# Sharing an attention kernel's exponentials between ScalarE and VectorE, in an order computed at build time

## Chip, cores and metric

The kernel runs on one core of one Trainium2 chip. The metric is the device time of one execution in microseconds (us), the median of several executions. The engines are PE (TensorE), ACT (ScalarE), DVE (VectorE) and POOL (GpSimd); PEld is PE's weight load, SP starts DMA transfers. PSUM is the memory that PE writes its sums to, in banks of 128x512 numbers here; the other engines read them from there. The profile adds, for one execution, every instruction's start and length and the clock that PE was granted (1.0 is full speed).

An execution is called slow when it lies more than 1.5% above the fastest one of the same kernel. Ratios below are the mean time of one kernel's fast runs over that of the kernel before in the same rounds, so they differ a little from the ratio of the medians that are quoted.

## The reference

A multi-head attention block and a bilinear feed-forward block read the same `x` (2048 x 512, bf16), and a sigmoid gate per row mixes them.

```python
g = sigmoid((x * gate_w).sum(-1, keepdims=True))
q, k, v = split(x @ wqkv)                  # 32 heads of 16 columns
p = softmax(q @ k.T * 16 ** -0.5)          # 32 heads x 2048 x 2048
a = (p @ v) @ wo
b = ((x @ w_gate) * (x @ w_up)) @ w_down   # 512 -> 1376 -> 512
out = g * a + (1 - g) * b
```

Softmax needs 32 x 2048 x 2048 exponentials. The matmuls of the feed-forward block and the projections need no exponentials and are used to fill PE's free time ("fills").

## The kernel before

Scores are computed transposed (keys on partitions, 512 queries in the free dimension), four heads at a time, each in its own strip of 32 rows of PE. A *score group* is four heads x 128 keys x 512 queries, four blocks of 128x512; there are 512 groups. Three blocks make a *span*: three score matmuls into three PSUM banks, then one exponential over 1536 columns by ScalarE. Two slots of three banks alternate. PV matmuls (probabilities times V) sum one group in four column strips of one bank; V carries columns of ones, so the softmax denominator comes out beside the result.

```python
def exp(i):                                   # every exponential is ScalarE's
    u0, n = spans[i]                          # n = 3 blocks, 2 in the last head group
    o_exp[i] = P.op("act", lambda a: a.activation(
        PT[:, r0 : r0 + n, :]..., psS[:, slot[i] : slot[i] + 512 * n], ACT.Exp, scale=0.25), deps)

def pv(e):                                    # one PV group: four heads side by side
    for j in range(4):
        pe.matmul(psO[32*j : 32*j+32, :], Vp[:, kt, 8*b + 2*j + p, :], PT[:, cell[4*e+j], :],
                  start=(kt == 0), stop=(kt == T - 1), tile_position=(0, 32*j))

for i in range(len(spans)):                   # the order: a fixed pattern with credits
    exp(i)
    scores(i + 2)
    ...                                       # PV of what is ready
    rate = 4.0 if first else (2.0 if chunk == 0 else 1.3)
    credit = min(credit + rate, 4.0)          # at most this many fill matmuls a span
    ...
```

The softmax here doesn't subtract the row's maximum and nothing guards it: scores larger than these inputs give would overflow.

## Time and profile before

The kernel before takes 1002.07 us (median of 4 runs, 994.84 to 1008.29).

| what | value |
|---|---|
| ScalarE busy | 94% of 998.0 us |
| exponentials of 1536 columns, start to start | 1.345 us |
| exponentials of 1024 columns, start to start | 0.917 us |
| PE busy / mean granted clock | 79% / 0.838 |
| VectorE busy | 16% |

The first fence is from the page of the kernel before: busy us by engine (with the share of the 998.0 us span), the busy share in 40 equal slices (digits are tenths; PEclk is the granted PE clock in tenths), and the chain of work and waits that ended last, by engine (a q marks an engine's sequencer).

```profile
PE 786.5 (79%) x5072; PEld 187.9 (19%) x5072; DVE 159.1 (16%) x260; ACT 939.2 (94%) x713; POOL 50.3 (5%) x41
...
PE   3787788888888787788877788778778777777797
...
DVE  1333332122211111111011112110000100000001
ACT  2677799999999999999999999999999999999998
...
PEclk9998899999997999998999999998557955555557
...
ACT 61%; issue 17%; PE 14%; DVE 4%; DMA 2%; SPq 0%; ACTq 0%; DVEq 0%
```

ScalarE is at 9 in nearly every slice after the start and makes up 61% of the chain that ended last: it is the bound. PE's clock, the PEclk row, falls to half speed in the last quarter while ScalarE stays at 9.

The next fence has groups of instructions by form: line, engine, operation, output and input tile, shapes, count, then busy us and mean ns of one, then idle time before them and its releaser. After it come two rows of the chain of waits in order of time (start, length, and a merged run of large exponentials), then a timeline row of ScalarE with small ones.

```profile
L541 ACT ACTIVATE PT<-psS 128x1536 bf16<-128x1536 f32 x661 | 894.4, 1688 | 44.7 <-PE psS L520 44.2
L520 PE MATMUL psS<-QT,KE 32*128 32x512 bf16 x2048 | 319.4, 455 | 156.3 <-ACT PT L541 144.0 <-DVE KE L275 1.7 <-DVE QT L296 0.8
...
L541 ACT ACTIVATE PT<-psS 128x1024 bf16<-128x1024 f32 x32 | 30.2, 1022 | 2.9 <-PE psS L520 2.9
```

```profile
827.70 4.03 ACT PT L541 x3
833.07 9.41 ACT PT L541 x7
```

```profile
956.87 3.77 ACT L541 ACTIVATE PT<-psS 128x1024 bf16<-128x1024 f32 x4 [0.38 <-PE psS L520]
```

One large exponential lasts 1688 ns but overlaps the next: in the chain seven take 9.41 us and three 4.03 us, so (9.41 - 4.03) / 4 = 1.345 us from start to start. Four small ones take 3.77 us, so (3.77 - 1.02) / 3 = 0.917 us. PE sat idle for 144.0 us before score matmuls, waiting for exponentials, but ScalarE for only 47 us waiting for PE.

The last view is busy time by stretch of the span: the stretch, its length, then for PE, PEld, DVE, ACT and POOL busy us and instruction count, then PE clock, DMA share and GB/s.

```profile
0.00:100.00 100.00, 66.33 (x435) 18.18 (x435) 30.49 (x53) 61.25 (x45) 12.32 (x11) 0.95 0.37 88
100.00:700.00 600.00, 488.99 (x3274) 123.25 (x3271) 112.35 (x176) 587.72 (x436) 26.59 (x21) 0.95 0.04 12
...
800.00:850.00 50.00, 38.05 (x226) 7.17 (x226) 1.89 (x4) 50.00 (x39) 2.53 (x2) 0.50 0.04 12
```

The first 100 us cost 39 us of ScalarE time. From 100 us on ScalarE is 98 to 100% busy in these stretches (95% in the first 100 us of them), at the full clock and at the half clock alike (800 to 850 us: clock 0.50, ScalarE 50.00 of 50.00 us).

### The profile page before, as it was taken

To read this page: it belongs to the slowest core of one execution; us is meant where nothing else is said; L and a number is where in the kernel's file an instruction comes from. 1 tells how busy PE (TensorE), PEld (TensorE's weight loads), DVE (VectorE), ACT (ScalarE), POOL (GpSimd) and SP (SyncE) were. 2 spreads that over 40 slices of the span, in tenths; PEclk is the share of its full clock that TensorE was granted. 3 is DMA by queue.
4 is the path that set the end of the run, shared out by engine and by line. 5 is a ranking of instruction groups with operands and counts; after the bars stand their busy time and mean duration, and the time that the engine had idled before them with its cause. 6 is when DMAs were issued, how large, how long until landed. Compare 5 with 4: busy or idle time off the path is not lost.

```text
span 998.0 us, 11864 instructions
## 1 busy us (share of the span) xinstructions
PE 786.5 (79%) x5072; PEld 187.9 (19%) x5072; DVE 159.1 (16%) x260; ACT 939.2 (94%) x713; POOL 50.3 (5%) x41
## 2 busy tenths in 40 slices
PE   3787788888888787788877788778778777777797
PEld 0222122222222222222212122121111111111111
DVE  1333332122211111111011112110000100000001
ACT  2677799999999999999999999999999999999998
POOL 4000000000000000000000000000000000000000
PEclk9998899999997999998999999998557955555557
DMA  7600000000000000000000000000000000000000
GB/s 147 191 12 1 12 12 11 3 11 12 12 12 23 22 4 9 12 12 12 13 12 22 12 11 12 12 12 12 1 11 17 28 12 12 12 1 11 12 12 21
DMA packets 29980, 19.91 MB, mean 20 GB/s; under 512 B 19464, under 2 KB 24936, under 8 KB 29928
## 3 DMA queue, kind: packets, MB, share of 16 engines
q1 hardware_dynamic: 26760, 17.59, 6.2%
q10 hardware_dynamic: 3168, 1.57, 0.8%
q8 instruction: 39, 0.64, 0.3%
q14 instruction: 13, 0.11, 0.0%
HBM read 14.45 MB, written 2.35 MB: 17 GB/s over the span
## 4 chain that ended last, share of the span: by engine, by line
ACT 61%; issue 17%; PE 14%; DVE 4%; DMA 2%; SPq 0%; ACTq 0%; DVEq 0%
ACT PT L541 60%; PE psS L520 4%; PE psO L563 3%; DVE KE L275 2%; PE psF L263 2%; PE psF L304 2%; DVE Vp L309 1%; DMA den<-oraw 1%; PE psF L350 1%; DMA xT<-in_A_x_dram 1%; PE psF L393 1%; PE psF L286 1%; PE psF L432 1%; ACT L718 1%; ACT L717 1%
## 5 line engine op out<-in xcount | busy, mean ns | idle before, releaser
L541 ACT ACTIVATE PT<-psS 128x1536 bf16<-128x1536 f32 (+1 forms) x694 | 925.0, 1657 | 47.6 <-PE psS L520 47.1
L520 PE MATMUL psS<-QT,KE 32*128 32x512 bf16 x2048 | 319.4, 455 | 156.3 <-ACT PT L541 144.0
L563 PE MATMUL psO<-PT,Vp 128*32 128x512 bf16 x2048 | 241.1, 461 | 5.1 <-DVE Vp L309 4.8
L520 PEld LDWEIGHTS psS<-QT,KE 32*128 32x128 bf16 x2048 | 69.2, 93 | 459.5 <-ACT PT L541 418.7
L617 POOL TENSOR_TENSOR OT<-oraw,rb 128x512 bf16<-128x512 f32 x31 | 39.2, 1266 | 909.1 <-DMA rb<-rscr 909.1
L563 PEld LDWEIGHTS psO<-PT,Vp 128*32 128x32 bf16 x2048 | 54.0, 95 | 157.5 <-issue 143.0
L350 PE MATMUL psF<-xT,wu 128*128 128x512 bf16 (+1 forms) x176 | 61.0, 408 | 9.2 <-DVE hT L381 7.4
L393 PE MATMUL psF<-wd,hT 128*128 128x512 bf16 (+1 forms) x176 | 62.9, 408 | 1.2 <-DVE bsb L399 1.1
L369 PE MATMUL psF<-xT,wg 128*128 128x512 bf16 (+1 forms) x176 | 58.8, 394 | 3.1 <-DVE usb L360 1.9
L595 DVE COPY oraw<-psO 128x512 f32<-128x512 f32 x31 | 21.4, 692 | 227.5 <-PE psO L563 227.2
L360 DVE CAST usb<-psF 128x512 bf16<-128x512 f32 (+1 forms) x44 | 30.2, 687 | 109.8 <-PE psF L350 109.8
L381 DVE TENSOR_TENSOR hT<-psF,usb 128x512 bf16<-128x512 f32 (+1 forms) x44 | 30.1, 684 | 96.1 <-PE psF L369 96.1
L263 PE MATMUL psF<-xT,wk 128*128 128x512 bf16 x64 | 22.0, 442 | 22.9 <-DMA xT<-in_A_x_dram 12.8
L432 PE MATMUL psF<-wo,OT 128*128 128x512 bf16 x96 | 36.2, 419 | 0.7 <-DVE ost L415 0.7
L399 DVE TENSOR_SCALAR bsb<-psF,omg 128x512 bf16<-128x512 f32 x16 | 11.9, 745 | 114.3 <-PE psF L393 114.3
L275 DVE TENSOR_SCALAR KE<-psF,mask 128x512 bf16<-128x512 f32 x32 | 22.5, 744 | 39.9 <-PE psF L263 39.9
L286 PE MATMUL psF<-xT,wq 128*128 128x512 bf16 x64 | 22.9, 426 | 3.1 <-DVE KE L275 2.4
L415 DVE SCALAR_TENSOR_TENSOR ost<-psF,gval,bsb 128x512 bf16<-128x512 f32 x13 | 9.8, 751 | 92.7 <-PE psF L432 87.6
L304 PE MATMUL psF<-wv,xT 128*128 128x512 bf16 x64 | 17.8, 403 | 2.1 <-DVE KE L275 1.4
L350 PEld LDWEIGHTS psF<-xT,wu 128*128 128x128 bf16 (+1 forms) x176 | 12.3, 100 | 38.0 <-issue 19.3
L393 PEld LDWEIGHTS psF<-wd,hT 128*128 128x128 bf16 (+1 forms) x176 | 13.0, 97 | 32.4 <-issue 27.2
L369 PEld LDWEIGHTS psF<-xT,wg 128*128 128x128 bf16 (+1 forms) x176 | 12.3, 99 | 30.6 <-issue 17.9
(42 smaller groups left out, 109.8 us busy)
## 6 DMA issues: line engine op xcount, KB each, us to landing
rb<-rscr SPq DMA_DIRECT2D x31, 256.0 KB
out_dram<-ost SPq DMA_DIRECT2D x16, 128.0 KB, 1.7
wu<-in_B_w_up_dram SPq DMA_DIRECT2D x1, 1376.0 KB, 6.4
wg<-in_B_w_gate_dram SPq DMA_DIRECT2D x1, 1376.0 KB, 9.3
wd<-in_B_w_down_dram SPq DMA_DIRECT2D x1, 1280.0 KB, 12.4
wv<-in_A_wqkv_dram ACTq DMA_DIRECT2D x1, 512.0 KB, 6.4
wo<-in_A_wo_dram SPq DMA_DIRECT2D x8, 64.0 KB, 7.9
den<-oraw SPq DMA_DIRECT2D x31, 8.0 KB
```

The costliest lines, as they stand in the source:

```text
L263: return pe.matmul(psF[:], wk[:, kt, b * 128 : (b + 1) * 128], xT[:, kt, ch * 512 : (ch + 1) * 512], start=s0, stop=s1,)
L275: lambda v, p=p: v.tensor_scalar(KE[:, p, b, ch * 512 : (ch + 1) * 512], psF[:], mask[:, p : p + 1], None, ALU.mult),
L286: return pe.matmul(psF[:], wq[:, kt, b * 128 : (b + 1) * 128], xT[:, kt, c * 512 : (c + 1) * 512], start=s0, stop=s1,)
L304: return pe.matmul(psF[:], xT[:, kt, t * 128 : (t + 1) * 128], wv[:, kt, :], start=s0, stop=s1)
L350: return pe.matmul(psF[0:w, :], wu[:, kt, f * 128 : f * 128 + w], xT[:, kt, c * 512 : (c + 1) * 512], start=s0, stop=s1,)
L369: return pe.matmul(psF[0:w, :], wg[:, kt, f * 128 : f * 128 + w], xT[:, kt, c * 512 : (c + 1) * 512], start=s0, stop=s1,)
L393: return pe.matmul(psF[:], hT[0:w, f, tt * 128 : (tt + 1) * 128], wd[0:w, f, :], start=s0, stop=s1)
L432: return pe.matmul(psF[:], OT[:, (NQ * c + g) % NOT, tt * 128 : (tt + 1) * 128], wo[:, g, :], start=s0, stop=s1)
L520: r = pe.matmul(psS[:, lo : lo + 512], KE[32 * j : 32 * j + 32, p, b, kt * 128 : (kt + 1) * 128], QT[32 * j : 32 * j + 32, c % 2, b, :], s ...
L541: lambda a: a.activation(PT[:, r0 : r0 + n, :].rearrange("p a b -> p (a b)"), psS[:, slot[i] : slot[i] + 512 * n], ACT.Exp, scale=0.25,),
L563: r = pe.matmul(psO[32 * j : 32 * j + 32, :], Vp[:, kt, 8 * b + 2 * j + p, :], PT[:, cell[4 * e + j], :], start=(kt == 0), stop=(kt == T - 1),
L617: lambda g: g.tensor_tensor(OT[:, m % NOT, :], oraw[:, s, :], rb[:, s, :], ALU.mult),
```

## The change

The intent is to take exponentials off ScalarE. The scores are scaled so that one doubling is 256 units. For some score groups VectorE clips the scores from PSUM to int16, then forms `0.5 * x + constant` as int16 and reads those bits as bf16. In bf16 one doubling is 128 units of the bit pattern, so this is a rough power of two, with straight lines between powers. Four such patterns, shifted against each other and weighted, come closer to the exponential. The weighted sum is left to PE: the four patterns are multiplied with four copies of V that carry the weights, all into the same PSUM sum. The price is four PV groups in place of one.

The change also rewrites the rest: one K copy instead of two masked ones (Q is split over rows instead), an output projection of half the matmuls, fills spread over almost the whole span, spans of two or three blocks (the third bank may hold VectorE's scores or a fill), and an order of instructions that is computed at build time from a small model of PE, ScalarE and VectorE with fixed durations.

```diff
+_OCT = 256.0
+_QSCALE = 0.25 / _LN2 * _OCT
+_OFF = [-7.25, 24.25, 55.75, 88.25]
+_WT = [1.0, 0.828125, 0.7109375, 0.60546875]
+DK = [3, 7, 11, 15]          # key tiles of a head group that VectorE may take
+D_START = 60.0               # model time of VectorE's first group
+FFN_FROM, FFN_TO = 75.0, 490.0
+MM = 0.2135                  # model: one PE slot; 0.105 more for a change of kind
 ...
+# VectorE, four times a group:
+v.tensor_scalar(I2[:, nb, j, :], bank, _LO, _HI, ALU.max, ALU.min)          # f32 -> int16
+# then four times a group, over 2048 columns:
+v.tensor_scalar(dstt, src, 0.5, _BASE + _OFF[k], ALU.mult, ALU.add)         # int16 -> int16
 ...
+# PE, for each of the four patterns k:
+pe.matmul(psO[32*j : 32*j+32, :], vcol(m, kt, k, j),                        # V times weight k
+          lview(e, k, j) if isd else PT[:, ring_e[e][j], :],                # bits read as bf16
+          start=first, stop=last, tile_position=(0, 32*j))
 ...
-for i in range(len(spans)):
-    exp(i)
-    ...
+steps = {"pe": step_pe, "act": step_act, "dve": step_dve}
+while st["pvg"] < NG or dve_q or active or fills:
+    eng = min(steps, key=lambda k: P.t[k])     # the engine that is free first in the model
+    if steps[eng](): ...
```

## The prediction

> **What bounds the kernel now.** ScalarE's exponentials. The page's busy line has ACT at 94% of 998.0 us; between 200 and 900 us the windows view shows it busy 97 to 100 us of every 100. The groups by form list 661 exponentials of 1536 columns and 32 of 1024. They overlap: in the timeline five large ones take 6.91 us (one starts every 1.344 us) and four small ones 3.77 us (every 0.917 us). They occupy about 661 x 1.344 + 32 x 0.917 = 918 us. The other 80 us are the start (first exponential at 19.6 us, then about 25 us of gaps until 100 us, waiting for PE) and the tail (last exponential ends near 981 us, eight table loads). PE is 79% busy, but waits for ACT (418.7 us before weight loads); VectorE is at 16%.
>
> **What the change moves.** By the built instruction lists, 96 of 512 score groups go to VectorE. ScalarE keeps 184 exponentials of 1536 columns and 556 of 1024: 184 x 1.344 + 556 x 0.917 = 757 us, 161 us less. Small spans are less efficient (0.459 against 0.448 us a block); their third bank now carries VectorE's scores or fills.
>
> **What it adds.**
> - VectorE: 384 clips (128x512, PSUM to int16) and 384 affine passes (128x2048 int16 in SBUF). A clip should cost what other evictions here do (0.69 us). For the pass no duration exists here; the Trainium skill, "VectorE: DVE Perf Modes", section on the perf-mode tier table, gives 693 ns for a 2048-column 16-bit tensor_scalar in 4x mode. Estimate: about 480 us added, 620 us in all, 70 to 80% of the new span: no bound, if int16 gets the 4x mode. At 1x (2.3 us) everything would be lost.
> - PE: PV groups rise from 528 to 816, fills fall from 848 to 788, score bursts number 740 instead of 694; 370 of 384 VectorE score matmuls ride behind a burst. At 0.2135 us a slot and 0.105 us a change of kind (timeline: 0.32 us between starts at a change), PE needs 2358 x 0.2135 + 1566 x 0.105 = 668 us, against 614 before.
>
> **Critical path.** All 161 us lie on it, but not all is kept. A score burst starts when the exponential two before ends and takes 0.39 us; with 1.344 us spans it had about 0.7 us to spare, with 0.917 us spans about 0.3 us, less than one PV slot plus its change. The order is fixed at build time, so any VectorE or PE slip stops an in-order engine. I expect ACT to lose 25 to 55 us to new waits. Start and tail stay similar. PE is denser and its fills last to the end, so the half-clock stretch after 720 us (clock 0.50) should mostly go.
>
> **Prediction: 868 us, range 830 to 920.** Chances: faster by over 2% 0.91, within 2% 0.05, slower 0.04.
>
> **What would show each step right or wrong.** ACT's exponentials sum to 757 us at these start-to-start times; ACT's waits for PE grow from 47 to 70-110 us; affine passes last about 0.7 us each; VectorE is 70-85% busy; mean PE clock is above 0.93; the chain of waits is shared among ACT, PE and VectorE.
>
> **What would make it wrong.** Affine passes not at 4x (over 1100 us); the clock at 0.5 for long stretches (PE-bound, over 930); an order so well matched that ACT hardly waits (about 830); VectorE's queue holding PE's banks, with waits for VectorE before PV and fills.

## The result and the profile after

The changed kernel takes 855.33 us (median of 4 runs, 846.01 to 859.96), against 1002.07 us. The ratio of the fast runs is 0.8507 (95% interval 0.8402 to 0.8611): faster, 13 us below the point predicted and inside the range.

Its profiled execution happens to be the slowest of the four (859.96 us, clock 0.928; the others had 0.932 to 0.952), just over the line to slow.

From the page of the changed kernel (span 858.1 us):

```profile
PE 774.0 (90%) x6164; PEld 200.7 (23%) x6164; DVE 628.9 (73%) x1010; ACT 778.7 (91%) x759; POOL 36.1 (4%) x34
...
PE   3777998899999999898999999998999999999895
...
DVE  1326689988989973787998479897967599896401
ACT  1427999999999998899999989999999999999997
...
PEclk9857969999999999889999999999999999999856
...
PE 38%; ACT 32%; DVE 16%; issue 7%; SPq 4%; DMA 3%; ACTq 0%; DVEq 0%
```

ScalarE, PE and VectorE are now busy 91, 90 and 73%, and the chain that ended last is shared: PE 38%, ScalarE 32%, VectorE 16%. PE's clock is high in the last quarter, where it used to be half, but for the last three slices. It is low in slices 2 to 4, and there ScalarE stands at 2 to 7.

Groups by form of the changed kernel:

```profile
L1259 ACT ACTIVATE PT<-psS 128x1024 bf16<-128x1024 f32 x556 | 535.4, 1137 | 19.0 <-PE psS L864 7.6 <-PE psO L987 6.3 <-PE psS L748 4.4
...
L1259 ACT ACTIVATE PT<-psS 128x1536 bf16<-128x1536 f32 x184 | 269.9, 1537 | 52.1 <-PE psS L748 47.4 <-PE psO L987 3.4 <-PE psX L864 0.9
L887 DVE TENSOR_SCALAR I<-psS 128x512 int16<-128x512 f32 x329 | 220.9, 685 | 35.7 <-PE psS L864 34.6
L918 DVE TENSOR_SCALAR LL<-I 128x2048 int16<-128x2048 int16 x288 | 194.6, 704 | 3.5 <-PE psO L987 2.0
...
L918 DVE TENSOR_SCALAR I<-I 128x2048 int16<-128x2048 int16 x96 | 70.1, 730 | 1.6
```

The affine passes over 2048 int16 columns last 0.70 to 0.73 us and the clips 0.685 us. The exponentials' busy time, overlaps counted once, fell from 925.0 us to 764.6 us on the two pages, by 160.4 us. The prediction had 161 us.

Who ScalarE waited for (us in all, times, longest), before and then after:

```profile
ACT PT L541 <- PE psS L520: 47.1, 55, 14.0
```

```profile
ACT PT L1259 <- PE psS L748: 51.7, 21, 14.6
ACT PT L1259 <- PE psO L987: 9.7, 6, 3.5
ACT PT L1259 <- PE psS L864: 7.6, 15, 1.5
```

That is 47.1 us before and 69.0 us after. By stretch, after:

```profile
0.00:100.00 100.00, 69.93 (x408) 17.27 (x408) 39.36 (x67) 48.77 (x42) 13.51 (x18) 0.78 0.35 89
100.00:820.00 720.00, 676.82 (x5599) 177.97 (x5598) 585.38 (x935) 696.98 (x686) 21.36 (x15) 0.97 0.07 18
```

ScalarE was idle for 38.8 us of the first 100 us before and for 51.2 us after: 12.5 us of the new loss lie in the start. From 100 to 820 us it is idle for 23 us. Before it was idle for 14.2 us between 100 and 960 us.

The sum over the two profiled executions: exponentials -160.4 us, ScalarE's idle time +20.6 us (58.8 to 79.4 us), together -139.8 us. The spans differ by 998.0 - 858.1 = 139.9 us. This is bookkeeping (a span is ScalarE's busy plus its idle time); it shows only that ScalarE's other work did not change.

### The profile page after: what moved, and what is told of

Same layout as the page of the kernel before. It is cut to its first block, busy times and chain, and to the rows that moved or that the text cites. A ratio compares the mean times of both kernels' runs of the same rounds, so it can differ in the third digit from the quotient of the medians.

```text
span 858.1 us, 15166 instructions
## 1 busy us (share of the span) xinstructions
PE 774.0 (90%) x6164; PEld 200.7 (23%) x6164; DVE 628.9 (73%) x1010; ACT 778.7 (91%) x759; POOL 36.1 (4%) x34
## 4 chain that ended last, share of the span: by engine, by line
PE 38%; ACT 32%; DVE 16%; issue 7%; SPq 4%; DMA 3%; ACTq 0%; DVEq 0%
ACT PT L1259 30%; PE psS L748 12%; PE psO L987 10%; DVE I L887 5%; DVE LL L918 5%; PE psX L504 3%; PE psX L426 3%; SPq L410 2%; PE psX L555 2%; DVE I L918 2%; PE psS L555 2%; SPq L1037 1%; DVE VV L434 1%; DMA xT<-in_A_x_dram 1%; PE psX L342 1%
## 5 line engine op out<-in xcount | busy, mean ns | idle before, releaser
L1259 ACT ACTIVATE PT<-psS 128x1024 bf16<-128x1024 f32 (+1 forms) x740 | 764.6, 1236 | 71.1 <-PE psS L748 51.7
L748 PE MATMUL psS<-QX,KT 32*128 32x512 bf16 x1664 | 300.5, 406 | 38.1 <-ACT PT L1259 27.6
L887 DVE TENSOR_SCALAR I<-psS 128x512 int16<-128x512 f32 x329 | 220.9, 685 | 35.7 <-PE psS L864 34.6
L918 DVE TENSOR_SCALAR LL<-I 128x2048 int16<-128x2048 int16 x288 | 194.6, 704 | 3.5 <-PE psO L987 2.0
L987 PE MATMUL psO<-PT,VV 128*32 128x512 bf16 x1664 | 163.9, 407 | 6.9 <-DVE VV L434 6.4
L748 PEld LDWEIGHTS psS<-QX,KT 32*128 32x128 bf16 x1664 | 71.1, 91 | 324.3 <-ACT PT L1259 257.2
L864 PE MATMUL psS<-QX,KT 32*128 32x512 bf16 x329 | 129.0, 392 | 0.2
L987 PE MATMUL psO<-LL,VD 128*32 128x512 bf16 x768 | 72.8, 397 | 0.5 <-DVE LL L918 0.4
L918 DVE TENSOR_SCALAR I<-I 128x2048 int16<-128x2048 int16 x96 | 70.1, 730 | 1.6
L504 PE MATMUL psX<-xT,wg 128*128 128x512 bf16 (+1 forms) x160 | 51.9, 400 | 1.1 <-DVE usb L518 0.9
L504 PE MATMUL psX<-xT,wu 128*128 128x512 bf16 (+1 forms) x148 | 50.0, 403 | 0.9 <-DVE hT L528 0.5
L864 PEld LDWEIGHTS psS<-QX,KT 32*128 32x128 bf16 x329 | 30.0, 91 | 1.7 <-DMA QX<-Qst 0.8
```

Of the source, the lines that this page charges most:

```text
L504: return pe.matmul(bk[0:w, :], ws[:, kt, f * 128 : f * 128 + w], xT[:, kt, c * 512 : (c + 1) * 512], start=s0, stop=s1,)
L748: q = pe.matmul(bank_ap(sl, k_), KT[32 * j : 32 * j + 32, b, kt * 128 : (kt + 1) * 128], QX[32 * j : 32 * j + 32, c % 2, p, b, :], start=True,
L864: lambda pe: pe.matmul(bank, KT[32 * j : 32 * j + 32, b, kt * 128 : (kt + 1) * 128], QX[32 * j : 32 * j + 32, c % 2, p, b, :], start=True, ...
L887: lambda v: v.tensor_scalar(I2[:, nb, j, :], bank, _LO, _HI, ALU.max, ALU.min),
L918: lambda v: v.tensor_scalar(dstt, src, 0.5, _BASE + _OFF[k], ALU.mult, ALU.add),
L987: r = pe.matmul((psD if dn else psO)[32 * j : 32 * j + 32, :], ones[:, k_, :] if dn else vcol(m, kt, k_, j), lview(e, k, j) if isd else PT ...
```

## The experiments

The account above says where time went, not what holds it. These theories were put to the test (E to H were formed after parts 1 and 2 below):

- A: the gain is the exponentials that left ScalarE; PE and VectorE have room.
- B: a good part of it is the rebuilt order and the fewer fills.
- C and D: PE slots, or VectorE's lateness, set the pace of the changed kernel.
- E: PE's clock matters. It falls to half when PE has little to do, and in the new order that costs time. F denies it.
- G: the start loses time to a single PSUM bank.
- H: the order pays only while the model's durations are right.

"Slots" below are PE's slots: one fill matmul, one score burst, one PV group of four strips, or one score matmul of VectorE that rides behind no burst, counted from the built instruction lists, at the 0.2135 us that they take at full clock.

### 1. No offload, and half of it

```diff
-D_START = 60.0
+D_START = 1e9                # d_off: no group ever goes to VectorE
```
```diff
-DK = [3, 7, 11, 15]
+DK = [7, 15]                 # d_half: 60 groups instead of 96
```

> All of the change except the offload: the new layouts, single K copy, halved output projection, fills spread to the end, build-time order, but no score group on VectorE (674 exponentials of 1536 columns and 13 of 1024, about 918 us at 1.344 and 0.917 us start to start). Theory A (the gain is the exponentials that leave ScalarE): 985 to 1010 us, within 2% of the kernel before. Rival B (a good part of the gain is the rebuilt order and the fewer fills): 960 us or less.

> VectorE may take two key tiles of a head group instead of four: 60 score groups move instead of 96; 418 exponentials of 1536 columns and 276 of 1024, about 816 us start to start. Theory A (ScalarE bound, the rest constant): 60/96 of the way from no offload, about 905 to 920 us. Rival C (PE or VectorE already bounds the changed kernel at 96): clearly less than proportional loss, 880 us or less.

`d_off` took 1046.93 us (median of three fast runs, 1037.42 to 1052.11; ratio 1.0416, interval 1.0346 to 1.0485), correct. B is wrong: without the offload, the rest of the change costs 4%. But A missed as well; it said at most 1010 us. The runs' mean clock was only 0.71 to 0.73, against 0.82 to 0.85 for the kernel before. `d_half` took 938.0 us (ratio 0.9342), 18 to 33 us more than A's range, at a clock of 0.85 to 0.86. So moving groups pays, and more than ScalarE's time explains: 109 us from `d_off` to `d_half`, for exponentials of 918 - 816 = 102 us, and 83 us from there to the changed kernel, for 816 - 757 = 59 us. That pointed to the clock.

One execution of `d_off`, the profiled one, took 2390.83 us. In its timeline of PE:

```profile
1003.55 1.34 PE L748 MATMUL psS<-QX,KT 32*128 32x512 bf16 x3
1004.83 1.35 PE L987 MATMUL psO<-PT,VV 128*32 128x512 bf16 x4
```

Two slots in a row start 1.28 us apart instead of 0.2135 us. That lasts until about 1935 us of the span; from there on it is 0.84 us (2302.97 and 2303.81 us in the same view). The trace holds no clock record of this execution at all: its page has no PEclk row, and the 1.000 that its run list gives only stands for that. No other run did this. Its cause is open and it is left out of the medians; for the same reason there is no profile of a usual run of `d_off`.

### 2. Less PE work

```diff
+nw = 64 if k_ else 512       # pv_narrow: patterns 1 to 3 multiply 64 columns (wrong result)
-(psO)[32*j : 32*j+32, :], ..., PT[...][:, :],
+(psO)[32*j : 32*j+32, 0:nw], ..., PT[...][:, 0:nw],
```

> Wrong result on purpose. Same order, same waits, but three of the four PV groups of a VectorE score group multiply 64 columns instead of 512, which takes some 0.187 us out of each of 288 PE slots, about 54 us of PE time. Theory A (ScalarE bound, order leaves PE room): 845 to 860 us, within 1% of the changed kernel. Rival C (PE slots set the pace): 800 to 835 us. A lower PE clock from the lighter load would be seen in the clock.

Its output is wrong, which doesn't matter for the time. From the view of the PV line (duration min/median/max in ns) of `pv_narrow`:

```profile
L989 PE MATMUL psO<-LL,VD x768: 192/203/261, 82.8 to 834.0; 128*32 128x64 bf16 x192
...
L989 PE MATMUL psO<-LL,VV x384: 379/391/634, 82.1 to 833.2; 128*32 128x512 bf16 x192
```

The narrowed matmuls take 203 instead of 391 ns, so by these durations 288 slots x 0.188 us = 54 us of PE work are gone, in the same order and with the same waits. The kernel took 890.25 us (883.20 to 892.49), ratio 0.8846 against 0.8507: with less to do for PE it became some 35 us **slower**. Both theories missed. Its mean clock was 0.85 to 0.88, and its PEclk row

```profile
PEclk9667557679969999688999996899998897999856
```

shows a low clock in many places where the changed kernel has 9. ScalarE's idle time before exponentials rose from 71.1 to 96.8 us on the two pages, 25.7 of the 32.6 us by which the spans differ. Of the theories listed, only E, not yet stated then, fits this.

### 3. More PE work

```diff
-for dn in range(2 if tail else 1):
+for rp, dn in [(rp, dn) for rp in range(2) for dn in range(2 if tail else 1)]:
     for j in range(4):
         pe.matmul(..., start=first and rp == 0, stop=last and rp == 1, ...)
```

Every PV group is issued twice. Numerator and denominator double together, so the result stays right. `d_off_pv2` does this to `d_off`, `before_pv2` does the same to the kernel before.

> The d_off kernel with the same order, but every PV group issued twice (numerator and denominator both double, so the result stays right): 512 more PE slots of 0.2135 us, 109 us more PE work and nothing else. Theory E (the new kernels lose time where the PE clock falls to 0.5, and dense PE work holds the clock up): the clock rises from 0.71 to above 0.85 and the time FALLS, to 990 to 1030 us. Rival F (the clock is a by-product, d_off is slow because its order is poor): 1050 us or more, since PE has more to do.

> The kernel before with every PV group issued twice (result stays right). Its ScalarE is nearly always busy, even at the half clock. Theory E says a higher clock brings it little beyond its start: 985 to 1005 us, within 2%, at a clock above 0.9. If the half clock cost the kernel before much, it would be 975 us or less; if PE work were critical there, 1020 us or more.

`d_off_pv2` took 1018.45 us (1007.71 to 1020.06), ratio 1.012 (1.005 to 1.019) against 1.0416: over 500 more PV groups made it 28 us **faster**, at a clock of 0.91 to 0.93. F is wrong. `before_pv2` took 1000.38 us, ratio 0.9965 (0.991 to 1.0021), at a clock of 0.92: the same. So the clock rose in the kernel before too, but there the higher clock and the added work together changed nothing. The PEclk rows of `d_off_pv2` and of `before_pv2`:

```profile
PEclk9659878799998999989999999799999999899988
```

```profile
PEclk9998999999999999999999989899969966767688
```

Ten kernels, by share of the span that their slots would fill at full clock (slots x 0.2135 us / median time; an estimate):

| kernel | slots | us | slot share | mean clock |
|---|---|---|---|---|
| d_off | 2003 | 1047 | 41% | 0.71 |
| before | 2070 | 1002 | 44% | 0.84 |
| pass_2x (below) | 2358 | 1136 | 44% | 0.77 |
| d_half | 2205 | 938 | 50% | 0.86 |
| pv_narrow | 2358, 288 of them narrow | 890 | 50% | 0.86 |
| fast_dve (below) | 2361 | 1010 | 50% | 0.87 |
| d_off_pv2 | 2531 | 1018 | 53% | 0.91 |
| before_pv2 | 2598 | 1000 | 55% | 0.92 |
| changed kernel | 2358 | 855 | 59% | 0.94 |
| late0 (below) | 2372 | 829 | 61% | 0.96 |

Roughly, the denser PE is, the higher its clock (at 44% there are 0.77 and 0.84). In general that is a correlation, since a slow kernel has a low share whatever slowed it. But in `pv_narrow`, `d_off_pv2` and `before_pv2` only PE's work was changed, the clock followed, and in the new order the time followed the clock.

### 4. Less and more VectorE work

```diff
-v.tensor_scalar(dstt, src, 0.5, ...)
+v.tensor_scalar(dstt[:, 0:1024], src[:, 0:1024], 0.5, ...)    # pass_half (wrong result)
```
```diff
-src = I2[:, nb, :, :].rearrange("p a b -> p (a b)")
+src = I2[:, nb, :, :].rearrange("p a (b t) -> p t (a b)", t=2) # pass_2x: every second column,
                                                                # then the rest; dstt alike
```

`pass_half` also narrows the clip's limits and clears `LL` once at the start, so that no unwritten or invalid pattern is read.

> Wrong result on purpose. Same order, but each of the 384 affine passes covers 1024 columns instead of 2048, some 0.27 us less each, about 100 us of VectorE time. Theory A: within 1% of the changed kernel (848 to 862 us). Rival D (VectorE lateness holds the in-order PE and through it ScalarE): 845 us or less.

> The changed kernel in the same order, with the affine passes walking their columns two apart (even ones, then odd ones; same result), which should put them out of the fastest mode: some 1.15 us a pass instead of 0.70, about 170 us more on VectorE, 800 us busy of a span of 855. Theory A says VectorE had 27% to spare, but the order was built for 0.6 us passes, so late passes now stop the in-order PE: 875 to 930 us. If the time stays within 1%, VectorE's timing hardly matters at all; if passes stay at 0.70 us the edit missed its mark.

The pass in `pass_half` (groups by form):

```profile
L919 DVE TENSOR_SCALAR LL<-I 128x1024 int16<-128x1024 int16 x288 | 114.5, 425 | 4.7 <-PE psO L988 3.1
```

425 ns instead of 704 ns, so about 108 us of VectorE time are gone; the kernel took 854.53 us (845.61 to 862.60), ratio 0.8484 (0.8433 to 0.8535), the same as the changed kernel's 0.8507. D is wrong for the passes: as long as they are now, they hold up nothing that shows within the interval. Shorter clips were not tried.

In the other direction, from the view of the pass line in `pass_2x` (durations in ns, then who waited for the passes, in us and times):

```profile
L918 DVE TENSOR_SCALAR LL<-I x288: 1290/1374/2237, 73.4 to 1073.3; 128x2048 int16<-128x2048 int16 x144
...
  PEld psO L987: 199.9, 255
  PE psO L987: 100.6, 162
```

A pass lasted 1374 ns (1.15 us had been expected) and the kernel 1135.82 us (ratio 1.1323, correct): the whole gain and 13% more were lost. That is far above the 875 to 930 us expected, although VectorE was busy for only 876 of 1131 us. PE's weight loads and matmuls waited for passes that came late (in the changed kernel the same two rows have 34.8 and 5.3 us); these waits overlap, and ScalarE waited for PE behind them (at 72% busy). PE, thinned out, fell to a clock of 0.77; how much of the loss is the clock's was not separated. VectorE had time to spare on average and none where the fixed order needed it.

### 5. The start

```diff
-if f is not None and f.due + F_LATE <= st["prog"] / 4 and ...:
+if f is not None and f.due + (F_LATE if now > 60 else 0) <= st["prog"] / 4 and ...:
```

> The changed kernel, but in its first 60 modelled us the projections of K and V may also take the third bank of a score slot at once, instead of only when six score groups late. In the profile of the changed kernel ScalarE has gaps of 3.9, 10.6 and 12.2 us before 65 us, while PE alternates one V projection and its eviction at the half clock in a single bank. Theory G (the start loses some 25 us to that one bank): 825 to 845 us. Rival (the start is bound by DMA arrival or by the half clock alone): 850 us or more.

ScalarE's timeline at the start, first in `tail` (a fast run whose start is the changed kernel's), then in `late0`; the bracket is the idle time before the row and its releaser:

```profile
22.90 1.45 ACT L1259 ACTIVATE PT<-psS 128x1536 bf16<-128x1536 f32 x1 [0.27 <-PE psS L748]
28.27 5.48 ACT L1259 ACTIVATE PT<-psS 128x1536 bf16<-128x1536 f32 x4 [3.92 <-PE psS L748]
44.42 5.58 ACT L1259 ACTIVATE PT<-psS 128x1536 bf16<-128x1536 f32 x4 [10.67 <-PE psS L748]
```

```profile
27.02 5.61 ACT L1259 ACTIVATE PT<-psS 128x1024 bf16<-128x1024 f32 x6 [0.65 <-PE psS L748]
35.24 5.61 ACT L1259 ACTIVATE PT<-psS 128x1024 bf16<-128x1024 f32 x6 [2.62 <-PE psS L748]
44.77 16.91 ACT L1259 ACTIVATE PT<-psS 128x1024 bf16<-128x1024 f32 x16 [3.92 <-PE psS L748]
```

The gaps of 3.92, 10.67 and (next row, not shown) 12.20 us became 0.65, 2.62 and 3.92 us. `late0` took 829.23 us (824.34 to 833.23), ratio 0.8256 (0.8203 to 0.8310), correct: some 26 us less than the changed kernel. The windows view between 24 and 66 us of the span, in `tail` and in `late0`:

```profile
24.00:66.00 42.00, 30.78 (x117) 6.84 (x117) 13.46 (x21) 15.21 (x12) 0.00 (x0) 0.58 0.35 117
```

```profile
24.00:66.00 42.00, 35.86 (x253) 10.69 (x254) 22.22 (x35) 34.22 (x35) 0.00 (x0) 0.96 0.38 124
```

ScalarE gained 19 us there, PE's clock is at 0.96 instead of 0.58, and 253 matmuls are recorded instead of 117. G holds, but with the second bank the clock rose too, and this run does not separate the two. Nor are the 26 us the start's alone: the order computed for `late0` hands 99 score groups to VectorE instead of 96, and the exponentials' busy time on its page is 756.9 us instead of 764.6.

### 6. The tail

```diff
+a1_ = P.op("act", lambda a: a.activation(lnd[:, :], psD[:, :], ACT.Ln), ...)   # once
 for tt in range(4):
-    a1_ = P.op("act", lambda a, cs=cs: a.activation(lnd[:, cs], psD[:, cs], ACT.Ln), ...)
     a2_ = P.op("act", lambda a, cs=cs: a.activation(rlast[:, cs], lnd[:, cs], ACT.Exp, scale=-1.0), [a1_])
```

> The changed kernel, with the last logarithm taken over all four column blocks at once before the four exponentials: two table loads at the end instead of eight, six loads of 1.28 us fewer, most of them in the last chain. Expected 7 to 9 us less than the changed kernel: 846 to 849 us beside a median of 855.

`tail` took 852.39 us, ratio 0.8489 (0.8442 to 0.8537), not to be told from the changed kernel by time alone. In the timelines the stretch from the first closing table load to the end shrank from 858.1 - 841.38 = 16.7 us to 854.1 - 840.15 = 14.0 us. The 7 to 9 us were too much: the exponentials are now done at 844.3 us, but PE, at the half clock (0.43 us a slot) until about 845 us, starts the last matmul of the first part of the output projection only at 846.3 us, and the last products follow.

`best` is `late0` with `tail`:

> late0 and tail together: the two are at opposite ends of the span, so their gains should add: 829 less 3 us, 823 to 829 us, the fastest of this study.

It took 825.91 us (median of 6 runs, 823.60 to 835.92), ratio 0.8264 (0.8225 to 0.8303), correct. That is 17.4% less than the kernel before by the ratio. Against `late0` alone (0.8256 in another set of rounds) no gain is resolved. From its page:

```profile
PEclk9997989999999999999999999999999999999986
```

### 7. The offload alone, once more

> No offload, but with both things that d_off lacked: the start of late0 and the doubled PV groups that hold the clock. 655 exponentials of 1536 columns, 41 of 1024, about 918 us start to start. If start and clock are all that d_off lost, it lands where the kernel before is, 985 to 1005 us, and the offload is then worth 160 to 175 us against late0. If it stays at 1010 us or more, something else in the new order costs too.

`d_off` with the edits of parts 3 and 5 (`d_off_late0_pv2`) took 993.28 us (983.01 to 996.78), ratio 0.9899 (0.9847 to 0.9950), correct, at a clock of 0.92 to 0.95. So the start and the clock explain what `d_off` lost against the kernel before. Against `late0` the offload is then worth 993 - 829 = 164 us. The exponentials on the page of `d_off_late0_pv2`, then on that of `late0` (both forms together; busy us, mean ns, idle before):

```profile
L1259 ACT ACTIVATE PT<-psS 128x1536 bf16<-128x1536 f32 (+1 forms) x697 | 922.6, 1557 | 35.7 <-PE psS L748 35.1
```

```profile
L1259 ACT ACTIVATE PT<-psS 128x1024 bf16<-128x1024 f32 (+1 forms) x741 | 756.9, 1242 | 45.5 <-PE psS L748 27.7
```

By these rows 165.7 us of exponentials left ScalarE with the 99 groups. A holds once the start and the clock are kept nearly equal (`late0` has 0.95 to 0.97).

### 8. A wrong model

```diff
-EV = dict(dur=0.6, lat=0.1)
+EV = dict(dur=0.3, lat=0.1)   # the model's time of an eviction; the passes' 0.6 likewise
```

> late0, but the model that builds the order is told that VectorE's evictions and passes take 0.3 us instead of 0.6. It then hands 108 score groups to VectorE instead of 99. Theory H (the order pays only while the model's VectorE time is right): 845 us or more, with waits for VectorE before scores and PV. Rival (the order is not delicate, and nine more groups at 1.6 us each are a gain): 805 to 825 us.

`fast_dve` moves 108 groups instead of 99 and took 1010.40 us (996.42 to 1017.43; ratio of the fast runs 1.0006, interval 0.9940 to 1.0072), correct. Nothing is left of the gain. Its profile is of a slow run (2.1% above the fastest); the largest waits for PE and VectorE in it are:

```profile
ACT PT L1259 <- PE psS L748: 114.4, 129, 13.6
...
ACT PT L1259 <- PE psS L864: 85.6, 112, 3.1
PEld psO L987 <- DVE LL L918: 84.2, 184, 1.8
```

ScalarE waited for scores 200 us in all, where it waited for 37 us in the profile of `late0`. H holds, more strongly than expected: the weight loads of PV groups waited 84 us for passes that the model believed done, and the scores stand behind them on PE. The clock fell too, from 0.96 to 0.87. The two changes of this run, the order and nine more groups, were not taken apart.

## Why the prediction was right

The prediction was right; these are its steps.

- **The bound and the work moved: right.** The exponentials' busy time fell by 160.4 us (predicted 161), and with clock and start kept nearly equal the offload of `late0`, 99 groups, is worth 164 us, for exponentials of 165.7 us.
- **VectorE: right for this order.** A clip took 0.685 us and a pass 0.70 to 0.73 us. The Trainium skill, "VectorE: DVE Perf Modes", section on the perf-mode tier table, gives 693 ns for bf16; the trace agrees, and shows that int16 gets that rate: 1024 columns more cost 704 - 425 = 279 ns, 3.7 columns per ns. VectorE is 73% busy (predicted 70 to 85). "No bound" was right for the time that the passes take (`pass_half`). But "at 1x everything would be lost" was too mild: already at 1.37 us a pass everything was lost.
- **New waits: right in kind, about half in size.** Predicted were 25 to 55 us; the idle time before exponentials (both forms together) rose from 47.6 to 71.1 us, by 23.5 us, and ScalarE's waits for PE from 47.1 to 69.0 us (plus 0.9 us in a row not shown; predicted 70 to 110). Half of the rise lies in the start (next point). The waits that the prediction argued for, behind short exponentials in the steady part, are fewer still: from 100 us to the closing part ScalarE's idle time rose from 14.2 to 23 us. So that the term is nearly of the predicted size is partly luck. The point of 868 us left 868 - (1002 - 161) = 27 us for all losses; the medians leave 14 us, the two profiled runs 20.6 us. Since runs of one kernel differ by 14 us, what the 13 us between 868 and 855 consist of is not shown.
- **"Start and tail stay similar": wrong for the start.** ScalarE lost 12.5 us more in the first 100 us, half of all new waits, and `late0` won 26 us, most of them there.
- **The clock: right in direction, missed in weight.** It is 0.93 to 0.95 and the half-clock stretch after 720 us is gone but for the end. The prediction counted the 288 extra PV groups as load only. `pv_narrow` shows that taking most of their work away costs about 35 us, with a clock that falls from 0.94 to 0.86. That their work pays here was luck: the prediction had not reckoned with it.
- **The chain of waits: right.** ScalarE's 61% became PE 38%, ScalarE 32%, VectorE 16%.
- **The fixed order: rightly called fragile.** The prediction took 25 to 55 us for slips. With a wrong duration in the model it is over 170 us (`fast_dve` against `late0`).

## What to carry to other kernels

Count the slots of the busiest engines before moving work: work for an engine with spare time is free only if the fixed order gives it that time where it is needed, so a build-time order must be fed with measured durations, and its tolerance tested by making one of them wrong. On PE, read the clock together with the busy share: here PE work that was taken out cost more than it saved (855 to 890 us), and useless PE work paid (1047 to 1018 us). Look at the start and the end of the span apart from the middle: a second bank in the first 60 us, with the three more groups that it let VectorE take, was worth 26 of 855 us.

## What the Trainium skill lacked or had wrong

- "TensorE: Matmul & The Clock Gate", section "What's actually happening", says that activity releases a throttle that grants half or the full rate. The traces agree: every clock record is 0.5 or 1.0. But the section "Why this matters for your kernels" names idle gaps over about 3 us as what costs the full clock. In the kernel before the clock was 0.50 from 800 to 950 us, and there the longest wait of a weight load was 1.2 us. These are consecutive rows of PE's matmuls there (start, length, idle before in brackets):

```profile
850.40 0.62 PE L563 MATMUL psO<-PT,Vp 128*32 128x512 bf16 x4
851.20 0.61 PE L520 MATMUL psS<-QT,KE 32*128 32x512 bf16 x3 [0.19 <-ACT PT L541]
852.55 0.61 PE L520 MATMUL psS<-QT,KE 32*128 32x512 bf16 x3 [0.74 <-ACT PT L541]
```

  The longest idle time is 0.74 us. The page's section "A second HAM failure mode: psum-queue depth-cycling" does tell of short, frequent idle times that made the clock swing between half and full; here it stayed at half for 150 us. The page gives no figure for how dense PE must be; here a mean clock above 0.9 went with slots filling 53% or more of the span, and one of 0.71 to 0.84 with 41 to 44%.
- The same page, section "Seeing it yourself", warns that the clock records can be unreliable and that a quarter rate was seen for more than 50 us. One run here had slots of 1.28 us, six times 0.2135 us, for some 1900 us and of 0.84 us, about four times, for the rest of its 2389 us, and no clock record at all. Whether that is the same thing is open.
- "VectorE: DVE Perf Modes", section on the perf-mode tier table, has columns for bf16 and fp32 and none for int16 (elsewhere the page speaks of 16-bit types in general); 2048 int16 columns took 0.70 us here, as the table has it for bf16. For 2x it has 1227 ns (fp32); int16 with columns two apart took 1374 ns, and which mode that was no run shows.
- "ScalarE: Activation LUTs", section "Table sets: the hidden batching unit", says that one set holds both the logarithm and the exponential and that a logarithm followed by an exponential needs one load. In this build every alternation of the two loaded a table, eight loads of 1.28 us at the end. The same page, "What ACT_TABLE_LOAD costs", adds a drain of about 1.38 us to each; in the timeline of the changed kernel the load from 841.38 us lasts 1.28 us and the logarithm starts at 842.67 us, so no such drain is seen here.
